# Row sums, low parts, weight conversions and a zero fill moved between engines in an attention, mixture-of-experts and bilinear kernel

## The chip, the core and the metric

The kernel runs on one core of one Trainium2 chip. The metric is the device time of one execution in microseconds (us). Three runs of the kernel before took 779.03, 779.79 and 782.46 us, so the median is 779.79.

## What is computed

The reference chains three layers. The bilinear weights reach the kernel as float64 and are converted in it.

```python
scores = scale * q @ k.T                     # 4 batches, 8 heads, 576 positions, head size 64
scores = where(0 <= rel < 128, scores + slope[h] * -abs(rel), -1e9)
attn = exp(scores - max);  attn /= attn.sum(-1) + 1e-9
x = (attn @ v)  ->  (2304 tokens, 512)
logits = x @ w_gate + modality_bias[modality_id]     # 8 experts, the best one is taken
out[mask] = gate_w[mask] * (relu(x[mask] @ w1[e]) @ w2[e])      # 512 -> 1024 -> 512
a = out @ w1;  b = out @ w2                  # 512 -> 1024 each
result = ((a * b) @ w3) @ w_out              # 1024 -> 1024 -> 512
```

## The kernel before, in words

**Number format.** Products that must be exact are made of split operands. ScalarE writes the high part (a rounded copy, `split` L270), VectorE the low part (source minus high part, L272, or L274 where a factor is applied), and `mm3` (L286 to L289) issues three matmuls: high by high (L287), high by low (L288) and low by high (L289).

**Stages.** From 0 to some 228 us the attention runs. From 262 us on come the experts' blocks and then the bilinear product, in which TensorE is busy nearly without a break. This change concerns the first stage and a few transfers for the second.

**Units.** The attention is cut into 4 batches of 5 chunks (four of 128 positions and a tail of 64), and each chunk into two units of four heads: 40 units, named (batch, chunk, unit). One iteration of the main loop issues scores and softmax of unit i, the transposes of the probabilities of unit i-1 and the product with v of unit i-2, so that three units are in flight. On every second iteration the queries and keys of the next chunk are transposed on TensorE (`transposes_q`, `transposes_k`) and split. The queries of two chunks in turn lie in the tiles qz0 and qz1.

**Low parts on TensorE.** For the chunks with `pe_lo` (of the first nine chunks the eight that aren't tails), the low part is not made by VectorE. TensorE multiplies the high part by a scaled negative identity (L281 for keys, L335 for queries) and adds it to the transposed source in PSUM, and ScalarE copies the rest out (L284, L341).

**Row sums.** The exponentials (L407) also give row sums, in another order of partitions than the tokens have. When the last unit of a chunk is attended, four GpSimd additions (L482) bring the sums of a 128-token tile into token order, `r`; VectorE takes the reciprocal (L486) and `gate_logits` multiplies by it (L511) before the token rows are stored.

**Routing.** Five times, after a group of tiles, `route` finds experts and ranks, and GpSimd issues one indirect DMA per tile (L577) that scatters token numbers into a table in device memory (`inv2`, shown as `inv`).

**Weights in between.** The product of w3 and w_out is worked in between the units: `W_STEPS` says how many steps of it (three matmuls each, `pw`) each unit carries. Their chunks are loaded as float64 words and converted by five VectorE instructions each in `to_f32`: three on words (L697, L701, L704) and two that sum (L707, L710). w_out's eight chunks are due at the units of `WO_AT`, loaded two units before; w3's chunks are loaded `LEAD[0]` units before their first step, converted `LEAD[1]` before and transposed `LEAD[2]` before. Then they are split like the queries.

**Order.** The program text gives each engine's instructions; a scheduler puts them into one order per engine, in which the engine then runs them strictly, each waiting for its semaphores.

**Zero fill.** `fill_rest` writes zeros over `yT`, the device-memory table of the experts' results, with one 128 by 512 tile of zeros, `zf`, one transfer per unit from unit 6 on; the first row of `zf` also becomes the zero row of the token table `xz`.

Of the kernel before, what the change touches and what calls it, by code (L numbers as in the profile page):

```python
# [8 lines left out]
F32 = mybir.dt.float32  # L9
# [9 lines left out]
P = 128  # L19
# [5 lines left out]
NB_MAX = 12  # L25
PE_LO = 9
WO_PRE, W3_PRE = 0, 0
WO_AT = [9, 9, 12, 12, 12, 12, 14, 15]
TP_AFTER = 20
LEAD = [4, 3, 1]  # L30
TS = 384
# [13 lines left out]
def kernel(  # L45
# [63 lines left out]
    ident = const.tile([P, P], F32, tag="ident", name="ident")  # L109
    id_k = a_p.tile([P, P], F32R, tag="id_k", name="id_k", bufs=1)  # L110
    id_q = a_p.tile([P, P], F32R, tag="id_q", name="id_q", bufs=1)
    ones_b = const.tile([P, P], BF16, tag="ones", name="ones_b")
# [65 lines left out]
    def build_constants():  # L178
# [7 lines left out]
        for t in qz[0]:  # L186
            nc.vector.memset(f32(t), 0.0)
        for t, f in ((id_k, -1.0), (id_q, 1.0 / SCALE)):
            nc.vector.tensor_scalar_mul(t, ident, f)

# [86 lines left out]

    def split_pe(hi, lo, tp):

        nc.scalar.activation(out=hi, in_=tp, func=AF.Copy)  # L280
        nc.tensor.matmul(  # L281
            tp, lhsT=id_k, rhs=hi, start=False, stop=True, skip_group_check=True,
        )
        nc.scalar.activation(out=lo, in_=tp, func=AF.Copy)  # L284

    def mm3(dst, lh, ll, rh, rl, start, stop):  # L286
# [9 lines left out]

    def pe_lo(b, c):
        return c < NF and b * (NF + 1) + c < PE_LO

    def head_transposes(nm, b, c, tp, hps):  # L300
        n_t = P if c < NF else TAIL
        t = raw[nm, b, c]
        for hp in hps:
            nc.tensor.matmul(
                tp[:, hp, :n_t],
                lhsT=t[:n_t, 2 * hp : 2 * hp + 2, :].rearrange("p a d -> p (a d)"),
                rhs=ident[:n_t, :n_t], is_transpose=True,
                start=(hp == hps[0] if pe_lo(b, c) else True),
                stop=(hp == hps[-1] or not pe_lo(b, c)),
            )  # L310

    def transposes_q(b, c, hps=range(NP)):
        tp = pst("A", [P, NP, P], f"qtp_{b}_{c}_{hps[0]}")
        head_transposes("q", b, c, tp, hps)
        n_h = 2 if c < NF else 1
        hi, lo = qT[b, c] = qz[(b * (NF + 1) + c) % 2]
        sl = slice(hps[0], hps[-1] + 1)
        parts = []
        for j in range(2):
            r = slice(j * D, (j + 1) * D)  # L320
            if n_h == 2:
                src = tp[r, sl, :].rearrange("p h (s q) -> p (h s) q", s=2)
                dst = [t[r, sl, :, r].rearrange("p h s q -> p (h s) q") for t in (hi, lo)]
            else:
                src = tp[r, sl, :HQ]
                dst = [t[r, sl, 0, r] for t in (hi, lo)]
            parts.append((r, src, *dst))
        if not pe_lo(b, c):
            for r, src, h, l in parts:
                split(h, l, src, scale=-SCALE)  # L330
            return
        for r, src, h, l in parts:
            nc.scalar.activation(out=h, in_=src, func=AF.Copy, scale=-SCALE)
        for j in range(2):
            nc.tensor.matmul(  # L335
                tp[:, sl, :].rearrange("p h (s q) -> p (h s) q", s=2), lhsT=id_q,
                rhs=hi[:, sl, :, j * HQ : (j + 1) * HQ].rearrange("p h s q -> p (h s) q"),
                start=False, stop=j == 1, skip_group_check=True,
            )
        for r, src, h, l in parts:  # L340
            nc.scalar.activation(out=l, in_=src, func=AF.Copy, scale=-SCALE)  # L341

    def transposes_k(b, c, hps=range(NP)):
# [9 lines left out]
        cs = slice(c * P, c * P + n_t)  # L353
        sp = split_pe if pe_lo(b, c) else split
        sp(hi[:, sl, cs], lo[:, sl, cs], tp[:, sl, :n_t])

# [85 lines left out]
    def attend(b, c, hq):  # L442
# [31 lines left out]
        if hq == NQ - 1:  # L474
            st_V.pop((b, c))
            if c < NF or b % 2 == 1:

                sm = sums.pop(i)
                r = a_p.tile([P, NP, 2], F32, tag="r", name=f"r_{b}_{c}", bufs=3)
                for h in range(2):  # L480
                    for j in range(2):
                        nc.gpsimd.tensor_scalar_add(  # L482
                            r[h * HQ : (h + 1) * HQ, :, j], sm[j * HQ : (j + 1) * HQ, h, :], 1e-9
                        )
                r = r.rearrange("p c j -> p (c j)")
                nc.vector.reciprocal(r, r)  # L486
                r_t[i] = r
# [197 lines left out]

    def to_f32(pool, raw_t, name, x=None):

        high = raw_t[:, :, 1]
        low = raw_t[:, :, 0].bitcast(U32)
        n = raw_t.shape[1]  # L690
        w = pool.tile([P, n], I32, tag="d_w", name=f"w_{name}", bufs=2)
        p2 = pool.tile([P, n], I32, tag="d_p", name=f"p_{name}", bufs=1)
        if x is None:
            x = pool.tile([P, HALF], F32, tag="d_x", name=f"x_{name}", bufs=3)

# [10 lines left out]
        )  # L706
        nc.vector.scalar_tensor_tensor(  # L707
            out=x, in0=low, scalar=2.0**-52, in1=p2.bitcast(F32), op0=ALU.mult, op1=ALU.mult
        )
        nc.vector.tensor_tensor(out=x, in0=x, in1=w.bitcast(F32), op=ALU.add)  # L710
        return x
# [8 lines left out]
    def load_wout(g):  # L720
        st_w["o", g] = load_f64(w_p, m_wout[g * P : (g + 1) * P], f"wo_{g}")

    def split_wout(g):
        x = to_f32(w_p, st_w.pop(("o", g)), f"wo_{g}")
        split(woh[:, g, :], wol[:, g, :], x)
# [6 lines left out]

    def cvt_w3(i):
        st_w["x", i] = to_f32(w_p, st_w.pop(("3", i)), f"w3_{i}")

# [61 lines left out]
    def fill_rest():  # L797
# [5 lines left out]
        nc.sync.dma_start(out=ord2.rearrange("(p n) o -> p (n o)", p=P), in_=ni[:, :n])  # L803
        zf = a_p.tile([P, DM], F32, tag="zf", name="zf", bufs=1)
        nc.gpsimd.memset(zf, 0.0)
        nc.sync.dma_start(out=xz[N : N + 1, :], in_=zf[:1, :])
        for j, (d, c) in enumerate((d, c) for c in range(0, NCOL, DM) for d in range(0, DM, P)):
            extras.setdefault(6 + j, []).append(
                lambda d=d, c=c: nc.sync.dma_start(
                    out=yT[d : d + P, c : min(c + DM, NCOL)], in_=zf[:, : min(DM, NCOL - c)]  # L810
                )
            )

# [42 lines left out]
    for g in range(NMC):  # L856
        if g >= WO_PRE:
            at(WO_AT[g] - 2, lambda g=g: load_wout(g))
        at(WO_AT[g], lambda g=g: split_wout(g))
# [51 lines left out]
    if j_in < n_j:  # L911
        load_w3(j_in)
        cvt_w3(j_in)
    if j_in + 1 < n_j:
# [160 lines left out]
    def cvt_m(q, i):  # L1075
# [4 lines left out]
        with tc.issue_after(last["w"].ins):  # L1080
            to_f32(cv_p, wc.pop(("m", q, i)), f"m_{q}_{i}", x=st_w["m"][:, slot, d % 2, :])

# [54 lines left out]
    for n in range(k_in, n_w):  # L1137
        j, first = w_piece(n)
        if first:
# [3 lines left out]
            if j + 1 < n_j:  # L1143
                cvt_w3(j + 1)
        w_step(n)
# [384 lines left out]
```

## Time and profile before

| | |
|---|---|
| Median of three runs | 779.79 us (779.03 to 782.46) |
| The profiled execution | 779.81 us, of which its span is 778.1 |
| Mean granted TensorE clock | 0.983 |
| Busy in the span: TensorE, VectorE, ScalarE, GpSimd | 740.4, 524.1, 363.9, 96.6 us |
| Bytes moved | 116.43 MB |

The shares of the whole span (95 % TensorE, 67 % VectorE) are a mean over stages that differ. The tables by stretch further down give the busy time of each engine in each stretch, with the granted clock as a share of full speed, the mean busy share of the DMA engines and their rate. In the names of rows PE is TensorE, PEld its weight load, DVE VectorE, ACT ScalarE, POOL GpSimd and SP the queue that issues most transfers. Small numbers behind an arrow name what an engine waited for.

### The profile page before, as it was taken

The numbers are of one execution on the slowest core, as the hardware profiler recorded it, in microseconds if no ns is written. First come the engines' busy times: TensorE is split into PE (matmuls) and PEld (weight loads), VectorE is DVE, ScalarE is ACT, GpSimd is POOL, SyncE is SP. The second block draws the span as 40 slices with busy tenths as digits, with TensorE's granted clock in tenths as the row PEclk, the third lists the DMA queues.
The fourth block names the chain that finished last, engine by engine and source line by source line (L and its number), as shares of the span: only waits on it lengthen the run. The fifth ranks groups of instructions, "written<-read, shape, count | busy, mean of one in ns | idle before, by whom it ended". The sixth has DMA issues, their size and how long they took to land. (4 is left out here: it accounts for less than half of the span.)

```text
span 778.1 us, 12375 instructions
## 1 busy us (share of the span) xinstructions
PE 740.4 (95%) x4296; PEld 641.0 (82%) x4296; DVE 524.1 (67%) x1314; ACT 363.9 (47%) x828; POOL 96.6 (12%) x171
## 2 busy tenths in 40 slices
PE   7899898979998999999999999999999999999996
PEld 6778676767876788888888878999789997899974
DVE  4679697737778649698894345788656786567721
ACT  5798776746871433333343435432542225423131
POOL 4100210300313402011020000000120001200011
PEclk9999999969999999999999999999999999999999
DMA  7998366234314857979696435644216332133011
GB/s 135 338 300 215 87 198 163 59 98 130 82 57 85 269 166 210 280 223 326 203 301 187 131 104 179 203 125 131 67 40 203 121 117 75 64 109 119 1 40 42
DMA packets 126166, 116.43 MB, mean 150 GB/s; under 512 B 69596, under 2 KB 100444, under 8 KB 126093
## 3 DMA queue, kind: packets, MB, share of 16 engines
q1 hardware_dynamic: 122477, 105.88, 46.4%
q0 software_dynamic: 3616, 9.66, 3.9%
q8 instruction: 36, 0.59, 0.3%
q14 instruction: 37, 0.30, 0.1%
HBM read 87.85 MB, written 27.68 MB: 148 GB/s over the span
## 5 line engine op out<-in xcount | busy, mean ns | idle before, releaser
L270 ACT ACTIVATE wth<-wt 128x896 fp32r<-128x896 f32 x48 | 43.0, 944 | 89.4 <-PE pP L1276 89.4
L272 DVE TENSOR_TENSOR fwl<-fw,fwh 128x1024 fp32r<-128x1024 f32 x40 | 48.7, 1225 | 52.0 <-ACT fwh L270 51.6
L270 ACT ACTIVATE fwh<-fw 128x1024 fp32r<-128x1024 f32 x40 | 42.2, 1062 | 82.6 <-PE ph L288 65.0
L407 ACT ACTIVATE p<-p,mn 128x192 f32<-128x192 f32 (+2 forms) x144 | 61.7, 431 | 13.6 <-DVE mn L402 13.0
L287 PE MATMUL ph<-xbh,fwh 128*128 128x480 f32 x160 | 61.4, 385 | 1.1 <-issue 0.7
L288 PE MATMUL py<-Whl,fwh 128*128 128x480 f32 x160 | 61.1, 382 | 0.0
L288 PE MATMUL ph<-xbl,fwh 128*128 128x480 f32 x160 | 60.9, 380 | 0.0
L289 PE MATMUL ph<-xbh,fwl 128*128 128x480 f32 x160 | 60.7, 380 | 0.0
L289 PE MATMUL py<-Whl,fwl 128*128 128x480 f32 x160 | 58.8, 379 | 0.0
L287 PE MATMUL py<-Whl,fwh 128*128 128x480 f32 x160 | 57.8, 380 | 0.0
L287 PE MATMUL po<-Whl,abh 128*128 128x512 f32 x144 | 57.2, 397 | 0.6 <-ACT abh L270 0.6
L289 PE MATMUL po<-Whl,abl 128*128 128x512 f32 x144 | 57.2, 398 | 0.0
L288 PE MATMUL po<-Whl,abh 128*128 128x512 f32 x144 | 57.0, 396 | 0.0
L272 DVE TENSOR_TENSOR wtl<-wt,wth 128x896 fp32r<-128x896 f32 x48 | 51.8, 1082 | 4.8 <-ACT wth L270 2.6
L402 DVE CUSTOM_DVE_ANT_0 p<-S,bias 128x192 f32<-128x192 f32 (+2 forms) x144 | 41.4, 329 | 20.1 <-PE S L289 18.3
L1381 POOL DMA_INDIRECT out_dram<-o,sid x18 | 21.6, 1201 | 260.4 <-ACT o L1380 260.4
L272 DVE TENSOR_TENSOR abl<-ab,abh 128x512 fp32r<-128x512 f32 x36 | 24.7, 690 | 41.0 <-ACT abh L270 40.9
L270 ACT ACTIVATE abh<-ab 128x512 fp32r<-128x512 f32 x36 | 22.5, 629 | 58.1 <-PE po L288 40.6
L1285 DVE TENSOR_TENSOR c<-pA,u 128x384 f32<-128x384 f32 x48 | 26.7, 557 | 33.8 <-PE pA L1276 31.6
L468 PE MATMUL av<-pT,vr 128*64 128x128 f32 (+2 forms) x576 | 46.9, 285 | 1.7 <-ACT pT L432 1.2
L468 PEld LDWEIGHTS av<-pT,vr 128*64 128x64 f32 (+1 forms) x576 | 32.3, 142 | 13.5 <-issue 5.7
L422 PE MATMUL PT<-ident,p 128*128 128x128 f32 x208 | 37.7, 299 | 4.5 <-ACT p L407 2.1
(251 smaller groups left out, 2009.0 us busy)
## 6 DMA issues: line engine op xcount, KB each, us to landing
wt<-wT SPq DMA_DIRECT2D x48, 448.0 KB
fw<-in_moe_w_dram SPq DMA_DIRECT2D x40, 512.0 KB
raw_w<-in_moe_w_dram SPq DMA_DIRECT2D x16, 512.0 KB
raw_m<-in_moe_w_dram SPq DMA_DIRECT2D x32, 256.0 KB
wT<-ms SPq DMA_DIRECT2D x16, 448.0 KB
yT<-zf SPq DMA_DIRECT2D x20, 256.0 KB
yT<-y SPq DMA_DIRECT2D x20, 240.0 KB
x<-yT SPq DMA_DIRECT2D x12, 384.0 KB
```

Source lines behind the costliest of these rows:

```text
L270: last["a"] = nc.scalar.activation(out=hi, in_=src, func=AF.Copy, scale=scale)
L272: last["v"] = nc.vector.tensor_tensor(out=lo, in0=src, in1=f32(hi), op=ALU.subtract)
L287: nc.tensor.matmul(dst, lhsT=lh, rhs=rh, start=start, stop=False)
L288: nc.tensor.matmul(dst, lhsT=lh, rhs=rl, start=False, stop=False)
L289: return nc.tensor.matmul(dst, lhsT=ll, rhs=rh, start=False, stop=stop)
L402: nc.vector.tensor_tensor_reduce(out=p[:, t, s, w0:], in0=S_t[s][:, t, w0:], in1=bias[:, hp, w0:], scale=1.0, scalar=BIG, op0=ALU.add, op1 ...
L407: nc.scalar.activation(out=p[:, t, s, w0:], in_=p[:, t, s, w0:], func=AF.Exp, scale=-1.0, bias=m1, accum_out=sm[:, col, hp : hp + 1],)
L422: nc.tensor.transpose(pt[:n, t, x, :], p[:, t, x * P : x * P + n], ident)
L468: nc.tensor.matmul(av[j * D : (j + 1) * D, hp, cs], lhsT=raw["v", b, cc][:n_k, 2 * hp + j, :], rhs=rhs, start=(i_k == 0), stop=(i_k == len ...
L1285: last["d"] = nc.vector.tensor_tensor(out=out, in0=in0, in1=in1, op=op)
L1381: sc = nc.gpsimd.indirect_dma_start(out=out, out_offset=bass.IndirectOffsetOnAxis(ap=sid[g][:, j, 0:1], axis=0), in_=o, in_offset=None, bo ...
```

## The change

Four things are changed, all in the attention stage's code.

1. The four GpSimd additions per tile that bring row sums into token order become two VectorE additions, where source and destination have the same partitions, and two ScalarE copies with an added constant, where they haven't. There are 18 tiles.
2. `split_pe`, `pe_lo` and their identities are gone. All queries and keys go through `split`: high part by ScalarE, low part by VectorE.
3. w_out's chunks are due one per unit, at units 8 to 15; each chunk's conversion (`words_wout`) stands one unit before its split, and its load three units before. w3's loads stand five units ahead and not four. The conversion tiles have one buffer more each (`d_w` 3, `d_p` 2). `to_f32` is cut in two functions; what they issue on VectorE is the same five instructions.
4. `yT` isn't filled with zeros: 24 transfers are gone. The zero row of `xz` comes from a part of a probability tile that stays zero.

```diff
-PE_LO = 9
-WO_AT = [9, 9, 12, 12, 12, 12, 14, 15]
+WO_AT = [8, 9, 10, 11, 12, 13, 14, 15]
-LEAD = [4, 3, 1]
+LEAD = [5, 3, 1]
...
-    def split_pe(hi, lo, tp):
-        nc.scalar.activation(out=hi, in_=tp, func=AF.Copy)
-        nc.tensor.matmul(
-            tp, lhsT=id_k, rhs=hi, start=False, stop=True, skip_group_check=True,
-        )
-        nc.scalar.activation(out=lo, in_=tp, func=AF.Copy)
...
-            parts.append((r, src, *dst))
-        if not pe_lo(b, c):
-            for r, src, h, l in parts:
-                split(h, l, src, scale=-SCALE)
-            return
-        for r, src, h, l in parts:
-            nc.scalar.activation(out=h, in_=src, func=AF.Copy, scale=-SCALE)
-        for j in range(2):
-            nc.tensor.matmul(
-                tp[:, sl, :].rearrange("p h (s q) -> p (h s) q", s=2), lhsT=id_q,
-                rhs=hi[:, sl, :, j * HQ : (j + 1) * HQ].rearrange("p h s q -> p (h s) q"),
-                start=False, stop=j == 1, skip_group_check=True,
-            )
-        for r, src, h, l in parts:
-            nc.scalar.activation(out=l, in_=src, func=AF.Copy, scale=-SCALE)
+            split(*dst, src, scale=-SCALE)
...
-        sp = split_pe if pe_lo(b, c) else split
-        sp(hi[:, sl, cs], lo[:, sl, cs], tp[:, sl, :n_t])
+        split(hi[:, sl, cs], lo[:, sl, cs], tp[:, sl, :n_t])
...
                 for h in range(2):
-                    for j in range(2):
-                        nc.gpsimd.tensor_scalar_add(
-                            r[h * HQ : (h + 1) * HQ, :, j], sm[j * HQ : (j + 1) * HQ, h, :], 1e-9
-                        )
+                    hs, os = (slice(k * HQ, (k + 1) * HQ) for k in (h, 1 - h))
+                    nc.vector.tensor_scalar_add(r[hs, :, h], sm[hs, h, :], 1e-9)
+                    nc.scalar.activation(
+                        out=r[hs, :, 1 - h], in_=sm[os, h, :], func=AF.Copy, bias=1e-9
+                    )
...
-        w = pool.tile([P, n], I32, tag="d_w", name=f"w_{name}", bufs=2)
-        p2 = pool.tile([P, n], I32, tag="d_p", name=f"p_{name}", bufs=1)
+        w = pool.tile([P, n], I32, tag="d_w", name=f"w_{name}", bufs=bufs)
+        p2 = pool.tile([P, n], I32, tag="d_p", name=f"p_{name}", bufs=bufs - 1)
...
+    def words_wout(g):
+        words = words_f32(w_p, st_w.pop(("o", g)), f"wo_{g}", 3)
+        st_w["xo", g] = sum_f32(nc.vector, w_p, words, f"wo_{g}")
...
     def split_wout(g):
-        x = to_f32(w_p, st_w.pop(("o", g)), f"wo_{g}")
+        x = st_w.pop(("xo", g))
         split(woh[:, g, :], wol[:, g, :], x)
...
-        zf = a_p.tile([P, DM], F32, tag="zf", name="zf", bufs=1)
-        nc.gpsimd.memset(zf, 0.0)
-        nc.sync.dma_start(out=xz[N : N + 1, :], in_=zf[:1, :])
-        for j, (d, c) in enumerate((d, c) for c in range(0, NCOL, DM) for d in range(0, DM, P)):
-            extras.setdefault(6 + j, []).append(
-                lambda d=d, c=c: nc.sync.dma_start(
-                    out=yT[d : d + P, c : min(c + DM, NCOL)], in_=zf[:, : min(DM, NCOL - c)]
-                )
-            )
+        nc.sync.dma_start(
+            out=xz[N : N + 1, :].rearrange("o (p c) -> (o p) c", p=4), in_=pTz[0][:4, 0, 1, :]
+        )
...
-            at(WO_AT[g] - 2, lambda g=g: load_wout(g))
+            at(WO_AT[g] - 3, lambda g=g: load_wout(g))
+        at(WO_AT[g] - 1, lambda g=g: words_wout(g))
         at(WO_AT[g], lambda g=g: split_wout(g))
```

Two places show what this makes of the engines' orders. The first is GpSimd around the scatters of the second group, of five tiles (the row sums r_1, r_2 belong to chunks 1 and 2 of batch 2; sums are the row sums as the exponentials left them; inv is the scatters' table). Before:

```order
L482 TENSOR_SCALAR r_1_2136<-sums_1864 64x4 [waits Activation_49]
L482 TENSOR_SCALAR r_1_2136<-sums_1864 64x4
L577 DMA inv_101<-tg,pos_i 19200x2 [waits DVE_49,Pool_49]
L577 DMA inv_101<-tg,pos_i 19200x2 x4
L482 TENSOR_SCALAR r_2_2287<-sums_2040 64x4 [waits Activation_49]
L482 TENSOR_SCALAR r_2_2287<-sums_2040 64x4 [waits DMASW6_49,DMASW5_49,DMASW7_49,DMASW4_49,DMASW0_49]
L482 TENSOR_SCALAR r_2_2287<-sums_2040 64x4 [waits Activation_49]
L482 TENSOR_SCALAR r_2_2287<-sums_2040 64x4
```

On the same engine after the change, the second group's five scatters follow the first group's, and the third group's begin right behind them:

```order
L545 DMA inv_99<-tg,pos_i 19200x2 [waits DVE_49]
L545 DMA inv_99<-tg,pos_i 19200x2 x3
L545 DMA inv_99<-tg,pos_i 19200x2 [waits DMASW0_49]
L545 DMA inv_99<-tg,pos_i 19200x2 [waits DMASW1_49,DVE_49]
L545 DMA inv_99<-tg,pos_i 19200x2 [waits DMASW2_49]
```

Before, the second addition of the row sums waits for five DMAs of GpSimd's own queue, the scatters; after, no row sum stands on that engine.

The second place is VectorE between the last softmax instruction of unit (0,2,1) and the first of unit (0,3,0) (w, p and x are the words, the power of two and the float32 value of a chunk of float64 weights, with _wo for w_out; wol is a low part of w_out, qz1l a low part of queries, lh and x<-xlg the gate's products and token rows; L402 is the softmax's first instruction). Before, from the first row behind the softmax of (0,2,1):

```order
L710 TENSOR_TENSOR x_wo_865<-x_wo_865,w_wo_863 128x512
L272 TENSOR_TENSOR wol<-x_wo_855,woh 128x512
L511 TENSOR_TENSOR lh_574<-xlg_0_575,r_1_554 128x32
L511 TENSOR_TENSOR x_573<-xlg_0_575,r_1_554 128x256
L511 TENSOR_TENSOR lh_574<-xlg_1_580,r_1_554 128x32
L511 TENSOR_TENSOR x_573<-xlg_1_580,r_1_554 128x256
L517 TENSOR_REDUCE lsum_585<-lh_574 128x8
L402 ISA p_3_0_604,mn_3_0_605<-S_3_0_0_589,bias 128x192
```

After the change 25 instructions stand in that place, with softmax now at L369; these are the last of them:

```order
L662 TENSOR_SCALAR w_wo_964<-raw_wo_788 128x512
L687 TENSOR_TENSOR x_wo_785<-x_wo_785,w_wo_780 128x512
L269 SCALAR_TENSOR_TENSOR qz1l<-qtp_3_0_472,qz1h 64x8x64
L669 TENSOR_SCALAR p_wo_852<-w_wo_851 128x512
L454 RECIPROCAL r_2_679<-r_2_679 128x8
L485 TENSOR_REDUCE lsum_564<-lh_553 128x8
L666 SCALAR_TENSOR_TENSOR w_wo_964<-raw_wo_788,w_wo_964 128x512
L662 TENSOR_SCALAR w_w_1_978<-raw_w_1_790 128x512
L267 TENSOR_TENSOR wol<-x_wo_785,woh 128x512
L681 SCALAR_TENSOR_TENSOR x_wo_856<-raw_wo_715,p_wo_852 128x512
L486 TENSOR_TENSOR logit_413<-lsum_564,bmod 128x8
L369 ISA p_3_0_587,mn_3_0_588<-S_3_0_0_572,bias 128x192
```

Before, seven instructions stand between two units' softmax there; after, 25, among them queries' low parts and parts of the conversions of three chunks of w_out and two of w3.

## Rows read from the trace of the kernel before

**Rows 1.** Busy time by stretch (first column its start and end).

```profile
core 0: us, PE busy (x) PEld busy (x) DVE busy (x) ACT busy (x) POOL busy (x), PEclk, DMA share, GB/s
0.00:36.00 36.00, 28.10 (x157) 23.54 (x158) 19.82 (x72) 23.78 (x70) 10.93 (x48) 0.95 0.85 223
36.00:92.00 56.00, 51.32 (x441) 42.83 (x440) 41.33 (x166) 47.02 (x144) 8.86 (x20) 0.97 0.77 214
92.00:129.00 37.00, 34.04 (x262) 26.44 (x261) 33.78 (x111) 25.01 (x77) 4.27 (x12) 1.00 0.63 178
100.00:120.00 20.00, 18.98 (x151) 14.61 (x152) 19.27 (x60) 13.68 (x45) 2.80 (x8) 1.00 0.67 190
...
162.30:175.00 12.70, 12.70 (x68) 11.95 (x69) 6.14 (x28) 7.47 (x26) 0.87 (x4) 0.52 0.33 84
...
262.00:778.00 516.00, 504.50 (x2501) 446.25 (x2499) 337.36 (x571) 187.49 (x277) 43.34 (x37) 1.00 0.47 147
```

**Rows 2.** Waits, 0 to 262 us: total us, times, longest.

```profile
DVE r L486 <- POOL r L482: 14.7, 8, 7.4
POOL r L482 <- DMA inv<-tg,pos_i: 12.6, 3, 6.5
```

**Rows 3.** Timeline from 160 us: start, duration; brackets hold idle time and releaser.

```profile
160.03 0.78 POOL L482 TENSOR_SCALAR r<-sums 64x4 f32<-64x4 f32 x3 [6.53 <-DMA inv<-tg,pos_i]
160.85 0.20 DVE L486 RECIPROCAL r<-r 128x8 f32<-128x8 f32 x1 [7.43 <-POOL r L482]
...
161.63 0.59 ACT L270 ACTIVATE qz1h<-qtp 64x512 fp32r<-64x512 f32 x1 [5.53 <-DVE qz1l L274]
...
162.28 0.53 PE L287 MATMUL S<-kTh,qz1h 128*128 128x192 f32 x1 [4.99 <-ACT qz1h L270]
```

**Rows 4.** Timeline of TensorE around low parts near 18 us and 40 us.

```profile
18.26 0.73 PE L281 MATMUL ktp<-kTh,id_k 128*128 128x512 f32 x1
...
19.64 0.57 PE L287 MATMUL S<-kTh,qz1h 128*128 128x192 f32 x2
...
39.63 0.64 PE L335 MATMUL qtp<-qz1h,id_q 128*128 128x512 f32 x2
40.11 0.49 PE L422 MATMUL PT<-ident,p 128*128 128x128 f32 x3
```

**Rows 5.** Groups by form, 0 to 262 us: busy us, mean ns, idle before.

```profile
L482 POOL TENSOR_SCALAR r<-sums 64x4 f32<-64x4 f32 x64 | 18.2, 284 | 156.4 <-ACT p L407 141.5 <-DMA inv<-tg,pos_i 12.6
...
L701 DVE SCALAR_TENSOR_TENSOR w_w<-raw_w,w_w 128x512 int32<-128x512 int32 x16 | 10.9, 684 | 0.2
...
L704 DVE TENSOR_SCALAR p_w<-w_w 128x512 int32<-128x512 int32 x16 | 6.8, 425 | 0.1
...
L272 DVE TENSOR_TENSOR kTl<-ktp,kTh 128x512 fp32r<-128x512 f32 x8 | 5.4, 679 | 0.9 <-ACT kTh L270 0.8
L341 ACT ACTIVATE qz1l<-qtp 64x512 fp32r<-64x512 f32 x8 | 4.7, 589 | 0.0
L541 ACT ACTIVATE ex<-dd 128x32 f32<-128x32 f32 x2 | 0.4, 216 | 0.0
L567 DVE TENSOR_SCALAR smx<-smx 128x4 f32<-128x4 f32 x2 | 0.3, 158 | 0.0
```

**Rows 6.** Timeline of VectorE, to 92 us, instructions on weights and softmax.

```profile
28.38 0.43 DVE L697 TENSOR_SCALAR w_w<-raw_w 128x512 int32<-128x512 int32 x1 [1.90 <-DMA raw_w<-in_moe_w_dram]
...
31.41 0.68 DVE L710 TENSOR_TENSOR x_w<-x_w,w_w 128x512 f32<-128x512 f32 x1
32.01 0.19 DVE L486 RECIPROCAL r<-r 128x8 f32<-128x8 f32 x1
...
35.96 0.36 DVE L402 CUSTOM_DVE_ANT_0 p<-S,bias 128x192 f32<-128x192 f32 x1 [0.72 <-PE S L289]
...
91.50 0.34 DVE L402 CUSTOM_DVE_ANT_0 p<-S,bias 128x192 f32<-128x192 f32 x1
```

**Rows 7.** Transfers issued, from the page's last part.

```profile
yT<-zf SPq DMA_DIRECT2D x20, 256.0 KB
```

More of the change, by code (lines that the diff above doesn't have):

```diff
@@ L109 @@
     ident = const.tile([P, P], F32, tag="ident", name="ident")
-    id_k = a_p.tile([P, P], F32R, tag="id_k", name="id_k", bufs=1)
-    id_q = a_p.tile([P, P], F32R, tag="id_q", name="id_q", bufs=1)
     ones_b = const.tile([P, P], BF16, tag="ones", name="ones_b")
@@ L187, in build_constants @@
             nc.vector.memset(f32(t), 0.0)
-        for t, f in ((id_k, -1.0), (id_q, 1.0 / SCALE)):
-            nc.vector.tensor_scalar_mul(t, ident, f)
         nc.gpsimd.iota(rel_i, pattern=[[-1, W]], base=P, channel_multiplier=1)
@@ L295 @@
     qT = {}
-    def pe_lo(b, c):
-        return c < NF and b * (NF + 1) + c < PE_LO
     def head_transposes(nm, b, c, tp, hps):
@@ L307, in head_transposes @@
                 rhs=ident[:n_t, :n_t], is_transpose=True,
-                start=(hp == hps[0] if pe_lo(b, c) else True),
-                stop=(hp == hps[-1] or not pe_lo(b, c)),
+                start=True, stop=True,
             )
@@ L317, in transposes_q @@
         sl = slice(hps[0], hps[-1] + 1)
-        parts = []
         for j in range(2):
@@ L684, in load_f64, with words_f32 @@
         return t
-    def to_f32(pool, raw_t, name, x=None):
+    def words_f32(pool, raw_t, name, bufs):
         high = raw_t[:, :, 1]
-        low = raw_t[:, :, 0].bitcast(U32)
         n = raw_t.shape[1]
-        w = pool.tile([P, n], I32, tag="d_w", name=f"w_{name}", bufs=2)
-        p2 = pool.tile([P, n], I32, tag="d_p", name=f"p_{name}", bufs=1)
-        if x is None:
-            x = pool.tile([P, HALF], F32, tag="d_x", name=f"x_{name}", bufs=3)
+        w = pool.tile([P, n], I32, tag="d_w", name=f"w_{name}", bufs=bufs)
+        p2 = pool.tile([P, n], I32, tag="d_p", name=f"p_{name}", bufs=bufs - 1)
         nc.vector.tensor_scalar(
@@ L706, in to_f32, with sum_f32 @@
         )
-        nc.vector.scalar_tensor_tensor(
-            out=x, in0=low, scalar=2.0**-52, in1=p2.bitcast(F32), op0=ALU.mult, op1=ALU.mult
-        )
-        nc.vector.tensor_tensor(out=x, in0=x, in1=w.bitcast(F32), op=ALU.add)
+        return raw_t, w, p2
+    def sum_f32(eng, pool, words, name, x=None):
+        raw_t, w, p2 = words
+        low = raw_t[:, :, 0].bitcast(U32)
+        if x is None:
+            x = pool.tile([P, HALF], F32, tag="d_x", name=f"x_{name}", bufs=3)
+        if eng is nc.vector:
+            eng.scalar_tensor_tensor(
+                out=x, in0=low, scalar=2.0**-52, in1=p2.bitcast(F32), op0=ALU.mult, op1=ALU.mult
+            )
+        else:
+            eng.tensor_scalar(out=x, in0=low, scalar1=2.0**-52, scalar2=None, op0=ALU.mult)
+            eng.tensor_tensor(out=x, in0=x, in1=p2.bitcast(F32), op=ALU.mult)
+        eng.tensor_tensor(out=x, in0=x, in1=w.bitcast(F32), op=ALU.add)
         return x
@@ L731, in load_w3, with cvt_w3 @@
         )
-    def cvt_w3(i):
-        st_w["x", i] = to_f32(w_p, st_w.pop(("3", i)), f"w3_{i}")
+    def cvt_w3(i, eng=nc.vector):
+        words = words_f32(w_p, st_w.pop(("3", i)), f"w3_{i}", 3)
+        st_w["x", i] = sum_f32(eng, w_p, words, f"w3_{i}")
     def w3_transposes(i):
@@ L803, in fill_rest @@
         nc.sync.dma_start(out=ord2.rearrange("(p n) o -> p (n o)", p=P), in_=ni[:, :n])
-        zf = a_p.tile([P, DM], F32, tag="zf", name="zf", bufs=1)
-        nc.gpsimd.memset(zf, 0.0)
-        nc.sync.dma_start(out=xz[N : N + 1, :], in_=zf[:1, :])
-        for j, (d, c) in enumerate((d, c) for c in range(0, NCOL, DM) for d in range(0, DM, P)):
-            extras.setdefault(6 + j, []).append(
-                lambda d=d, c=c: nc.sync.dma_start(
-                    out=yT[d : d + P, c : min(c + DM, NCOL)], in_=zf[:, : min(DM, NCOL - c)]
-                )
-            )
+        nc.sync.dma_start(
+            out=xz[N : N + 1, :].rearrange("o (p c) -> (o p) c", p=4), in_=pTz[0][:4, 0, 1, :]
+        )
     halves = [(slice(0, H // 2), range(NP // 2)), (slice(H // 2, H), range(NP // 2, NP))]
@@ L912 @@
         load_w3(j_in)
-        cvt_w3(j_in)
+        cvt_w3(j_in, nc.vector)
     if j_in + 1 < n_j:
@@ L1080, in cvt_m @@
         with tc.issue_after(last["w"].ins):
-            to_f32(cv_p, wc.pop(("m", q, i)), f"m_{q}_{i}", x=st_w["m"][:, slot, d % 2, :])
+            words = words_f32(cv_p, wc.pop(("m", q, i)), f"m_{q}_{i}", 2)
+            sum_f32(nc.vector, cv_p, words, f"m_{q}_{i}", x=st_w["m"][:, slot, d % 2, :])
     def sum_m(q, i):
@@ L1143 @@
             if j + 1 < n_j:
-                cvt_w3(j + 1)
+                cvt_w3(j + 1, nc.vector)
         w_step(n)
```

## The prediction

> **What bounds the kernel now.** I read the table of stretches first. From 262 us to the end TensorE is busy for 504.50 of 516.00 us at a clock of 1.00 [rows 1]. What the change moves all lies before that, and the instructions of these later stages stand in the same order in both kernels, so I cost them at nothing and carry whatever the attention gains or loses through to the end, us for us. The attention is not one regime. From 0 to 36 us no engine is busy for more than 28.10 us and the DMA engines for 0.85 of the time. From 36 to 92 us TensorE's matmuls are busy for 51.32 of 56 us, ScalarE 47.02, VectorE 41.33: TensorE leads and VectorE has 14.7 us to spare. From 92 to 129 us TensorE has 34.04 of 37 and VectorE 33.78; inside it, from 100 to 120 us, VectorE is at 19.27 of 20.00, a share of .964. That is the best share that VectorE reaches, and shows what it looks like as the bound.
>
> The list of waits then shows a stall of another kind [rows 2]: VectorE waits 14.7 us in all for GpSimd's row sums, and GpSimd, three times, 12.6 us for the scatters' DMAs. The timeline at 160 us shows the longest [rows 3]. GpSimd waits 6.53 us for scatters before it writes r, VectorE's reciprocal has then waited 7.43 us, behind it stands a low part of queries, behind that ScalarE's next high part (5.53 us late), and so TensorE stands idle for 4.99 us. What follows is dearer than the wait: from 162.30 to 175.00 us the granted clock is 0.52 (the 1.2 GHz level), with TensorE busy in every one of the 12.70 us [rows 1].
>
> **Row sums off GpSimd.** Removed are 72 GpSimd additions of some 284 ns [rows 5], and with them the place where a row sum queues behind scatters. Nothing that anyone waits for is then left behind the scatters in the order. At 160 us the 4.99 us of idle time go. If TensorE doesn't stand idle there, the clock need not fall: 12.70 us of work at 0.52 is 12.70 x 0.52 = 6.6 us at full clock, 6.1 us less. Together -11.1 us. What is late next: the reciprocal now waits for ScalarE, which carries half of the additions behind its exponentials. Added are 36 VectorE additions of some 158 ns and 36 ScalarE ones of some 216 ns (the nearest rows, L567 and L541, are of like width [rows 5]), 5.7 and 7.8 us in all. Spread over 18 tiles they are 0.75 us a tile; VectorE and ScalarE have room behind the stall (6.14 and 7.47 of 12.70 us busy [rows 1]), so I charge +1, between 0 and 2. So this stretch gives -10, with ends at -12 (nothing is charged and the idle time's tail goes too) and -4 (only the idle time goes).
>
> **Low parts off TensorE.** TensorE loses 27 matmuls, one for each group of ScalarE's copies: nine for keys and eighteen for queries, seven and fourteen of them 512 wide. Three of them take 19.64 - 18.26 = 1.38 us at the early clock, and two take 40.11 - 39.63 = 0.48 us at full clock [rows 4], 0.24 each. ScalarE loses 27 copies of up to 589 ns. VectorE gains 27 low parts; the full-width ones, 679 ns each [rows 5], start 32.01 - 31.41 = 0.60 us apart where another instruction of this size is followed at once [rows 6]. These are not added to the path one by one; they count in the stages' sums below.
>
> **Conversions.** The five instructions per chunk are the same, and only their place changes, in the order of VectorE. Before the first softmax instruction of unit (0,2,0) five instructions with two inputs (684 ns) and three with one (425 ns [rows 5]) fewer stand now: 3.4 + 1.3 = 4.7 us. Between that point and unit (1,2,0) 21 and 14 more stand. I take these counts from the orders of both kernels, the times from the trace.
>
> **The start, 0 to 35.96 us** (first softmax of unit (0,2,0) [rows 6]). VectorE gets twelve low parts of half or full width and four additions, some 6.6 + 0.6 us, and loses the 4.7 us of conversions and a wait of 1.90 us for a raw weight [rows 6]: level. TensorE loses the equal of six full-width low parts at half clock, 2 x 1.38 = 2.8 us, and two ScalarE copies that stood in the same chain go with each set. The zero fill is 20 transfers of 256 KB and four of half that, 5.8 MB [rows 7] (the four by the size of their tile in the program), issued from unit 6 on, when the stretch moves 223 GB/s with the engines 0.85 busy [rows 1]; 5.8 MB at that rate are 26 us of transfer time that no longer compete with loads. Its issues leave SP's queue too. How much of it was late for anyone the trace shows only at the 1.90 us. Bounds: 0 if all this was hidden, and -7 if TensorE's 2.8, the 1.9 and some 2.3 (half of the conversions) all count; I take -4, near the row that is seen in full.
>
> **36 to 92 us.** Here the sign of the change is decided. VectorE gets twelve full-width low parts and 21 conversions of two inputs, 33 x 0.60 = 19.8 us by starts; 14 with one input, 14 x 0.425 = 6.0; eight additions, 8 x 0.158 = 1.3. That is 27.1 us, and 29.7 by durations (33 x 0.68). VectorE then has 41.33 + 27 = 68.3 us of work between two points that lay 91.50 - 35.96 = 55.5 us apart [rows 6]. TensorE's 51.32 and ScalarE's 47.02 both sink, so VectorE is the bound. At its share of .964 the stretch takes 68.3 / .964 = 70.9 us, +15.4. In this sum the short wait for row sums inside the stretch is already gone. Bounds: 66.7 us at a share of 1.00 and 1.6 us fewer, +11; 68.3 / .85 = 80.4, +25, if the low parts' chain (ScalarE's high part, VectorE's low part, ScalarE's second, VectorE's second, as both write the same tile) leaves holes like that at 100 to 120 us four times over.
>
> Here a row and a page can be weighed. By matmul busy time TensorE fills 51.32 of 56 us, but its weight loads only 42.83 [rows 1]. The Trainium skill ("Trainium Kernel Development and Optimization", Best Practices) holds matmul busy time to be a bad measure, because matmuls are pipelined, and the share of weight loads a good one. By the first, TensorE had 4.7 us of room before, by the second 13.2; by the second, the matmuls taken away here were hidden, and the whole of VectorE's +15.4 stands against nothing. The sum above is made without either.
>
> **92 to 129 us.** The conversions that went ahead are missing here: some 11 us of VectorE's 33.78 go (counts from the orders, times as above). VectorE then has 22.8 us, and TensorE is next: its matmuls are busy for 34.04 of 37.0 us, its weight loads for 26.44 [rows 1]. So the gain lies between 37.0 - 34.0 = 3 and 37.0 - 26.4 = 10.6; I take -7, the middle, as the rows give no nearer one.
>
> **Sum.** -4 + 15.4 - 7 - 11.1 + 1 = -5.7. The profiled execution took 779.81 us with a span of 778.1, within 0.02 of the median 779.79, so I predict 779.8 - 5.7 = 774.1, rounded 774. All dear ends together give 0 + 25 - 3 - 4 = +18, all cheap ends -7 + 11 - 10.6 - 12 = -19; neither is likely as a whole.
>
> **Rivals.**
>
> *No change of note: the clock falls anyway.* The idle 4.99 us are gone, but another wait (the reciprocal behind ScalarE's exponentials) comes in the same place, and the stretch at 0.52 stays. Then -4 + 15.4 - 7 - 5.0 + 1 = +0.4, 780.2. For it: VectorE's order is strict, and ScalarE, at 47.02 of 56 us [rows 1], often runs late. Against: ScalarE loses more than it gets, and a row sum on it waits for exponentials alone, not for a DMA.
>
> *Slower: VectorE as the bound.* Place: 36 to 92 us. The work is put there, and a share of .85 in place of .964 gives 80.4 us, so that the sum becomes -4 + 25 - 7 - 10.1 = +3.9, 783.7; with a start that gains only 1, 786.7. I price it at 785. It decides from a share of about .90: 68.3 / .90 = 75.9 us, +20.4, eats all of the other 21.1 less 0.7. For it: 41.33 us before held many waits, and in a 20 us stretch with the same mix the share .964 was seen only once. Against: conversions wait for nothing but their loads, and fill holes.
>
> *Slower: the clock in the VectorE-bound stretch.* TensorE, left with some 45 to 50 us of work in 70, has gaps again and again; if each makes the clock fall as the one at 160 us did, two such stretches of 12.7 us cost 2 x 6.1 = 12.2 us, of which the bound by VectorE hides a third: +8, 782. For it stands the row at 0.52 behind one gap of 4.99 us; against it the stretch from 100 to 120 us, bound by VectorE, at 1.00 [rows 1]. The Trainium skill ("TensorE: Matmul & The Clock Gate", HAM oscillation) tells of kernels whose repeated waits let the clock fall each time and speaks for this rival; the rows at 100 to 120 us do not agree with it.
>
> **How the numbers follow.** About 0.5 %, 3.9 us, is what can be told from no change here: 775.9 to 783.7 is the same. My forecast has .50, with an own range of 767 to 778; .40 of it lies below 775.9 and .10 above. The clock that falls anyway has .17 and is the same. VectorE at .85 has .25, the clock in its stretch .08, both counted as slower, as their ranges lie about and above 783.7. Faster .40, same .27, slower .33. The range 765 to 790 leaves some .1 on either side out: below, if every term gains at its end but one; above, if the share falls under .80.
>
> **What would show it.** In the profile after: no L482, and the scatters of GpSimd with nothing behind them; around 160 us no idle time of TensorE over 2 us, and no stretch at a half clock behind it. VectorE busy for 65 us or more between the first softmax of unit (0,2,0) and that of (1,2,0), and these about 71 us apart; 80 or more would be the rival. The stretch from (1,2,0) to (2,0,0) shorter by some 7 us, with TensorE leading. The stretch from 262 us on the same length as before within 1 us. If that changes, the argument fails at its first step.

## The result, and the profile after

Five runs of the kernel after gave 784.26 to 789.33 us, median 785.21; five of the kernel before on the same chip 776.40 to 782.46, median 779.03. The ratio is 1.0089 (95 % interval 1.0060 to 1.0119): slower by 0.9 %, where 774 and faster had been forecast. The profiled execution after has a span of 783.4 us.

The forecast's stretches, cut at the same four points (VectorE's first softmax instruction of units (0,2,0), (1,2,0), (2,0,0) and (3,4,0)), compare as follows; each of the two columns of times is one profiled execution.

| Stretch | before | after | change | forecast |
|---|---|---|---|---|
| start to (0,2,0) | 35.96 | 29.46 | -6.5 | -4 |
| to (1,2,0) | 55.54 | 68.82 | +13.3 | +15.4 |
| to (2,0,0) | 37.26 | 33.16 | -4.1 | -7 |
| to (3,4,0) | 97.23 | 93.38 | -3.8 | -10.1 |
| to the end | 552.11 | 558.58 | +6.5 | 0 |
| sum | 778.10 | 783.41 | +5.3 | -5.7 |

The first three rows together were forecast at +4.4 and came to +2.7. The fault lies in the last two. The table of stretches of the kernel after answers to [rows 1]; its columns are the same:

```profile
core 0: us, PE busy (x) PEld busy (x) DVE busy (x) ACT busy (x) POOL busy (x), PEclk, DMA share, GB/s
0.00:29.46 29.46, 22.64 (x124) 20.29 (x125) 20.59 (x73) 17.53 (x58) 8.17 (x39) 1.00 0.82 176
29.46:98.28 68.82, 53.29 (x438) 44.30 (x436) 65.79 (x221) 45.35 (x145) 1.54 (x2) 0.90 0.64 166
98.28:131.44 33.16, 31.84 (x255) 26.44 (x255) 25.73 (x99) 24.16 (x77) 2.77 (x3) 1.00 0.55 128
131.44:224.82 93.38, 85.94 (x763) 72.37 (x763) 65.99 (x297) 72.80 (x252) 8.63 (x9) 1.00 0.45 100
237.00:241.50 4.50, 0.41 (x2) 0.00 (x0) 2.02 (x11) 0.21 (x1) 0.00 (x0) 0.78 0.33 76
241.50:250.00 8.50, 7.79 (x26) 5.92 (x27) 5.22 (x29) 1.21 (x3) 1.91 (x2) 0.51 0.20 62
```

In the second row VectorE is busy for 65.79 of 68.82 us, a share of .956: it is the bound, as forecast. In the fourth the clock is 1.00 throughout, so the stretch at half clock of [rows 1] is gone. The last two rows show TensorE all but idle for 4.5 us at 237 us, then 8.5 us at half clock. The kernel before has a smaller stall at the same place, the last routing step: TensorE waits 1.00 us there, and 3.5 us at half clock follow.

```profile
240.26 0.18 PE L559 MATMUL rk<-hot_b,tri_b 128*128 128x16 bf16 x1 [1.00 <-DVE hot_b L550]
```

```profile
243.00:246.50 3.50, 3.50 (x11) 2.68 (x10) 2.14 (x13) 0.00 (x0) 2.01 (x2) 0.53 0.52 137
```

The waits show why it grew (VectorE, 0 to 262 us, answering to [rows 2]):

```profile
engine line waited for: us in total, times, longest us
DVE w_w L662 <- DMA raw_w<-in_moe_w_dram: 14.5, 9, 3.7
DVE kTl L267 <- ACT kTh L265: 6.8, 7, 1.8
DVE lh L479 <- PE xlg L473: 5.9, 10, 1.8
DVE r L449 <- ACT p L374: 5.0, 9, 1.4
```

The 14.7 us for GpSimd's row sums have gone (5.0 us for ScalarE's exponentials stand ahead of the new row sums), and 14.5 us for loads of float64 weights have come. Before, VectorE had one such wait, 1.90 us [rows 6]. The timeline of one of the two longest, on VectorE and on the queue SP:

```profile
151.37 0.69 DVE L681 SCALAR_TENSOR_TENSOR x_w<-raw_w,p_w 128x512 f32<-128x512 uint32 x1
...
158.64 0.43 DVE L662 TENSOR_SCALAR w_w<-raw_w 128x512 int32<-128x512 int32 x1 [3.63 <-DMA raw_w<-in_moe_w_dram]
...
159.71 0.20 DVE L454 RECIPROCAL r<-r 128x8 f32<-128x8 f32 x1
```

```profile
152.09 0.35 SPq L651 DMA_DIRECT2D raw_w<-in_moe_w_dram  x1
```

L681 is the last reader of a load tile. 0.03 us after its end, at 152.09, the load of a later chunk into that tile is issued, and the next conversion in VectorE's order is of that very chunk: it stands 3.63 us, with the reciprocal behind it. The same happens at 193 us (3.65 us) and again from 236 to 239 us. There the last routing step is queued behind the conversion (VectorE, then TensorE):

```profile
236.02 0.17 DVE L486 TENSOR_TENSOR logit<-lsum,bmod 128x8 f32<-128x8 f32 x1
239.41 0.43 DVE L662 TENSOR_SCALAR w_w<-raw_w 128x512 int32<-128x512 int32 x1 [3.23 <-DMA raw_w<-in_moe_w_dram]
239.76 0.16 DVE L505 TENSOR_REDUCE mx<-logit 128x2 f32<-128x16 f32 x1
...
241.31 0.17 DVE L518 TENSOR_TENSOR hot_b<-iota_em,mnx 128x16 bf16<-128x16 f32 x1
```

```profile
241.54 0.19 PE L527 MATMUL rk<-hot_b,tri_b 128*128 128x16 bf16 x1 [4.13 <-DVE hot_b L518]
```

The last token's logits are ready at 236.2 us, but their maximum (L505) is taken at 239.76, behind a conversion that it has nothing to do with. TensorE waits 4.13 us for the routing's result, and the clock falls as it did at 162 us before.

Why does the order put the conversion there? The orders of both kernels tell. Both have three load tiles. Before, there were two word tiles (`d_w`); the words of chunk j+2 could be made only when chunk j was summed, and the load for it had long been issued, when chunk j-1 gave its tile free. With three word tiles the words of chunk j+3 may follow as soon as chunk j is summed, but that chunk's load waits for the same event. For the last seven chunks of w3, 27 to 106 VectorE instructions stand between a load tile's last reader and the first conversion from it in the kernel before, and by its trace 8.3 to 31.9 us; in the kernel after, 5 to 14 instructions and 3.7 to 7.3 us, the waits included. The count alone sets no threshold: at 114 and 118 us the kernel before has 16 and 18 instructions there, 6.8 and 6.5 us, and no wait.

### The profile page after: what moved, and what is told of

It is laid out like the page before. It is cut to its first block, busy times and chain, and to the rows that moved or that the text cites. A ratio compares the mean times of both kernels' runs of the same rounds, so it can differ in the third digit from the quotient of the medians.

```text
span 783.4 us, 12247 instructions
## 1 busy us (share of the span) xinstructions
PE 734.5 (94%) x4269; PEld 637.7 (81%) x4269; DVE 542.4 (69%) x1375; ACT 358.1 (46%) x837; POOL 72.9 (9%) x98
## 5 line engine op out<-in xcount | busy, mean ns | idle before, releaser
L435 PE MATMUL av<-pT,vr 128*64 128x128 f32 (+2 forms) x576 | 45.1, 277 | 8.5 <-ACT pT L399 4.7
L369 DVE CUSTOM_DVE_ANT_0 p<-S,bias 128x192 f32<-128x192 f32 (+2 forms) x144 | 41.4, 329 | 3.9 <-PE S L276 3.3
```

Source lines behind the costliest of these rows:

```text
L369: nc.vector.tensor_tensor_reduce(out=p[:, t, s, w0:], in0=S_t[s][:, t, w0:], in1=bias[:, hp, w0:], scale=1.0, scalar=BIG, op0=ALU.add, op1 ...
L435: nc.tensor.matmul(av[j * D : (j + 1) * D, hp, cs], lhsT=raw["v", b, cc][:n_k, 2 * hp + j, :], rhs=rhs, start=(i_k == 0), stop=(i_k == len ...
```

## The experiments

Three theories are told apart: **W**, the word tiles let the order run up against the loads; **B**, VectorE is the bound from 36 to 92 us; **P**, the new places of the conversions and their loads. Wherever the word tiles go from three to two or back, the power tiles go from two to one or back with them; "word tiles" stands for both, and which of the two decides isn't shown. Ratios are to the kernel before in runs on the same chip. On the three chips of these runs that kernel took 781.3 to 781.6 us.

**Word tiles back to two.**

```diff
-        words = words_f32(w_p, st_w.pop(("o", g)), f"wo_{g}", 3)
+        words = words_f32(w_p, st_w.pop(("o", g)), f"wo_{g}", 2)
-        words = words_f32(w_p, st_w.pop(("3", i)), f"w3_{i}", 3)
+        words = words_f32(w_p, st_w.pop(("3", i)), f"w3_{i}", 2)
```

> The kernel after, with its word tiles of the weight conversions back at two buffers and its powers at one, as before the change (load tiles three in both); nothing else differs. Theory W (waits for loads): with three word tiles on three load tiles, the order lets VectorE ask for a chunk right after the load tile it lands in came free, so VectorE stands 14.5 us for loads before 262 us, three times 3.2 to 3.7 us, the last time ahead of the last routing step. Expects these waits under 3 us in all and 775 to 780 us. Rival B (VectorE is the bound from 36 to 92 us, by low parts and conversions put there): the waits may go, but the time stays at 784 to 787. Rival P (placement: w_out one per unit, w3 loaded five units ahead): 784 to 787 as well.

773.67 us, ratio 0.9896 (0.9862 to 0.9931). VectorE has one wait left for such a load:

```profile
engine line waited for: us in total, times, longest us
...
DVE w_wo L662 <- DMA raw_wo<-in_moe_w_out_dram: 1.1, 1, 1.1
```

The size of these buffers decides the sign: 1.9 % between this and the kernel after. W holds; B and P, by which the time would stay, fall as the whole cause.

**Four load tiles, word tiles at three.** `load_f64(..., bufs=3)` becomes `bufs=4`.

> The kernel after with four load tiles in place of three for the float64 weights, word tiles at three as in the kernel after. Theory W: the loads are issued one chunk earlier, so VectorE's waits for loads fall from 14.5 us to under 3 and the time to 775 to 780 us, like the run with two word tiles. Rivals B and P: 784 to 787. If this one falls and the run with two word tiles doesn't, the number of loads in flight counts and not the distance in the order.

778.95 us, ratio 0.9968 (0.9948 to 0.9987). The waits go here too (0.5 us left), and some 9 us of the kernel after with them. But 5 us are missing against the run with two word tiles, and the stretch to (1,2,0) shows where (first this kernel, then the one with two word tiles):

```profile
29.63:98.72 69.09, 55.95 (x439) 45.83 (x438) 67.28 (x223) 45.54 (x145) 3.36 (x4) 0.88 0.67 171
```

```profile
30.13:93.31 63.18, 54.39 (x440) 44.49 (x439) 62.52 (x215) 44.78 (x145) 0.99 (x1) 0.89 0.67 174
```

VectorE is the bound in both (67.28 of 69.09, 62.52 of 63.18). With three word tiles the order pulls more conversions into it: 223 VectorE instructions in place of 215, among them nine more of conversions. So the third word tile costs twice: by late loads, and by work drawn into the stretch that VectorE bounds; in the second part B was right.

**Low parts back on TensorE**, as the diff of the change reversed in `transposes_q`, `transposes_k` and `split_pe`.

> The kernel after with the low parts of the first eight full chunks' queries and keys back on TensorE and ScalarE, and nothing else undone. Rival B: VectorE loses 27 low parts, some 17 us of work, most of it in the stretch from (0,2,0) to (1,2,0), which falls from 68.8 us towards 60; 775 to 779 us. Theory W: that stretch gets shorter by some 5 to 8 us at most, but the waits for loads at 155, 193 and 236 us and what follows them stay; 779 to 784.

792.28 us, ratio 1.0153 (1.0115 to 1.0192): neither theory's number. The stretch to (1,2,0) does shrink, from 68.8 to 66.7 us, but the waits for loads double:

```profile
DVE w_w L695 <- DMA raw_w<-in_moe_w_dram: 28.9, 11, 7.1
```

With word tiles at three this comparison says little of low parts; it is repeated with two below.

**Row sums back on GpSimd**, the four additions of before in `attend`.

> The kernel after with the row sums back as four GpSimd additions per tile. If the removed stall was worth what the prediction said of its stretch (10 us), 793 to 796 us, with TensorE idle again behind row sums around 150 to 165 us and a stretch at the lower clock. If the gain was only the 3.8 us that the stretch from (2,0,0) to (3,4,0) really lost, 787 to 791. If ScalarE's half of the sums makes up for it: 784 to 787.

792.52 us, ratio 1.0162 (1.0130 to 1.0195): 0.7 % slower than the kernel after by the first ratio of that kernel (1.0089), some 6 us, and 0.6 % by its later one (1.0102, below), whose interval overlaps this one. As a difference this is the second case (2 to 6 us); the time itself lies between the first two. The waits for loads (12.7 us) and for row sums (13.2 us) stand side by side in it.

**The kernel before with three word tiles and nothing else.**

```diff
-        w = pool.tile([P, n], I32, tag="d_w", name=f"w_{name}", bufs=2)
-        p2 = pool.tile([P, n], I32, tag="d_p", name=f"p_{name}", bufs=1)
+        w = pool.tile([P, n], I32, tag="d_w", name=f"w_{name}", bufs=3)
+        p2 = pool.tile([P, n], I32, tag="d_p", name=f"p_{name}", bufs=2)
```

> The kernel before with three word tiles and two power tiles for the weight conversions in place of two and one, nothing else. Theory W: VectorE's order then asks for chunks of w3 right behind the load tile's release here too (6 to 15 instructions between the two late in the attention, where before has 26 to 104), so VectorE waits for loads, about 10 us in all, also ahead of the last routing step: 785 to 791 us where before is 779 to 781. If the waits need the other changes too (w_out one per unit, low parts on VectorE): 778 to 783.

791.23 us, ratio 1.0119 (1.0072 to 1.0166). The tiles alone make the kernel before as much slower as the whole change did; the intervals overlap. The edit reaches the conversions of the bilinear product too, which the change left at two tiles, but the bilinear product takes 289.4 us in the profiles with and without it. The waits, in a profile of the slowest of its six runs (799.1 us):

```profile
DVE r L486 <- POOL r L482: 20.4, 7, 9.8
...
DVE w_w L697 <- DMA raw_w<-in_moe_w_dram: 13.4, 6, 5.3
```

Shown from both sides, then: taken out of the kernel after, and put into the kernel before. The loads are not all of it here: VectorE's waits for the row sums grew too, from 14.7 to 20.4 us.

**Two word tiles, and one part undone each.** These three have the first experiment's edit and the reversal named.

Low parts back on TensorE:

> The kernel after with two word tiles, as in the run that took 773.7 us, and the low parts of the first eight full chunks back on TensorE and ScalarE. If moving low parts to VectorE gains (its 27 instructions fit beside others, TensorE's 27 and ScalarE's 27 don't): slower than 773.7, 777 to 783. If it costs, as the prediction's stretch from 36 to 92 us has it (+15.4 us, about half of it by low parts): 765 to 770.

776.66 us, ratio 0.9940 (0.9914 to 0.9967). The interval overlaps that without the reversal, so no gain or loss is shown. The stretch to (1,2,0) takes 55.2 us in place of 63.2, the one from the start to (0,2,0) 37.4 in place of 30.1: the low parts on VectorE give ahead of (0,2,0) what they take behind it. The zero fill is absent from both, so what the start gained comes from the low parts.

Row sums back on GpSimd:

> The kernel after with two word tiles, and the row sums back as GpSimd additions. The prediction puts the row sums' move at 10.1 us (the idle time at 160 us and the clock behind it, less 1 us): 782 to 786. With three word tiles the same step cost about 4 us: 777 to 779 if that is what it is worth.

779.90 us, ratio 0.9970 (0.9932 to 1.0008), about 6 us slower than without the reversal, between the two expectations; the two intervals only just part.

Zeros back:

> The kernel after with two word tiles, and the 24 transfers of zeros back. If these transfers (5.8 MB from 20 to 44 us) delay loads that VectorE or TensorE wait for, 777 to 781. If they ran beside everything: 773 to 775, with the first units where they are without them.

778.20 us, ratio 0.9947 (0.9911 to 0.9984), overlapping; inconclusive. In its profile the unit (3,4,0) starts at 218.5 us, against 216.2 without the zeros; the start to (0,2,0) takes 29.5 us, against 30.1, so the zeros delayed nothing there.

**The kernel after once more, as it is.**

> The kernel after as it is, beside the next three on one chip, so that they can be set against it. All theories: 1.006 to 1.012 of the kernel before, and again over 10 us of VectorE's waits for loads of float64 weights before 262 us.

792.41 us, ratio 1.0102 (1.0057 to 1.0148), with 19.5 us of waits for loads. In this profile the stretch from (2,0,0) to (3,4,0) took 100.7 us where the first profile has 93.4. Its two waits for loads are longer there, 4.25 and 5.05 us in place of 3.63 and 3.65, and behind them the clock fell, which it did not in the first profile (the whole stretch, then a part of it):

```profile
159.42 0.43 DVE L662 TENSOR_SCALAR w_w<-raw_w 128x512 int32<-128x512 int32 x1 [4.25 <-DMA raw_w<-in_moe_w_dram]
```

```profile
161.91 0.35 PE L274 MATMUL S<-kTh,qz1h 128*128 128x192 f32 x1 [1.97 <-ACT qz1h L265]
```

```profile
131.59:232.28 100.69, 92.80 (x764) 78.94 (x763) 65.85 (x298) 73.43 (x252) 8.63 (x9) 0.92 0.43 93
165.00:175.00 10.00, 10.00 (x60) 9.43 (x59) 4.05 (x22) 6.58 (x24) 0.00 (x0) 0.55 0.42 102
```

**Two word tiles and four load tiles.**

> The kernel after with two word tiles and four load tiles; the instructions' order is that of the run with two word tiles and three load tiles. Theory W: with two word tiles no load was late any more, so a fourth load tile brings nothing: within 0.4 % of that run (a ratio of 0.986 to 0.994 to the kernel before). If the loads in flight were the scarce thing by themselves, under 0.985.

774.50 us, ratio 0.9905 (0.9869 to 0.9941): as with three load tiles. Where the order leaves time for a load, one more tile for it brought nothing.

**The conversions' old places.** Word tiles at two, and:

```diff
-WO_AT = [8, 9, 10, 11, 12, 13, 14, 15]
+WO_AT = [9, 9, 12, 12, 12, 12, 14, 15]
-LEAD = [5, 3, 1]
+LEAD = [4, 3, 1]
...
-            at(WO_AT[g] - 3, lambda g=g: load_wout(g))
-        at(WO_AT[g] - 1, lambda g=g: words_wout(g))
+            at(WO_AT[g] - 2, lambda g=g: load_wout(g))
+        at(WO_AT[g], lambda g=g: words_wout(g))
```

> The kernel after with everything on the weight conversions as before the change: w_out due at units 9, 9, 12, 12, 12, 12, 14, 15 and loaded two units before, w3 loaded four units ahead, two word tiles; row sums, low parts and zeros as in the kernel after. If the new places of the conversions were worth something: over 776 us, a ratio above 0.994. Theory W holds only the word tiles guilty and the places for nearly nothing, since the order moves by three instructions or fewer: a ratio of 0.986 to 0.994.

780.45 us, ratio 0.9981 (0.9951 to 1.0011). W's expectation missed: the new places are worth some 0.8 %, with the new low parts and row sums in place. They are a gain, so P is not what made the kernel after slower. In the one profile this kernel reaches (3,4,0) at 217.2 us, against 216.2 with the new places, and loses 3.1 us behind it. Why it is slower there stays open.

**The kernel before with the row sums moved, and nothing else.**

> The kernel before with the row sums moved from GpSimd to VectorE and ScalarE, and nothing else. The prediction's step says -10.1 us, 769 to 773 (a ratio of 0.985 to 0.990). By what the row sums cost when put back into the kernel after (about 4 to 6 us): 774 to 778 (0.992 to 0.996). If another wait takes the stall's place: a ratio of 0.997 to 1.003.

770.73 us, ratio 0.9864 (0.9829 to 0.9900), the fastest of all. Its stretches, cut as in the table above:

```profile
0.00:36.37 36.37, 29.64 (x162) 24.88 (x163) 20.32 (x76) 24.80 (x75) 8.66 (x40) 1.00 0.86 221
36.37:89.91 53.54, 48.70 (x416) 41.19 (x414) 42.03 (x173) 48.08 (x150) 4.21 (x4) 0.97 0.77 221
89.91:127.10 37.19, 34.26 (x285) 27.90 (x284) 34.61 (x118) 27.05 (x84) 0.00 (x0) 1.00 0.66 182
127.10:214.82 87.72, 83.21 (x736) 69.97 (x735) 66.06 (x297) 72.53 (x251) 9.12 (x9) 1.00 0.51 106
```

The first three stretches are those of the kernel before within 2 us (36.0, 55.5, 37.3); the fourth takes 87.72 in place of 97.23, at a clock of 1.00. By the ratio the step is worth 10.6 us, where the prediction has 10.1. It and the kernel after with two word tiles (0.9896; 0.9905 with four load tiles) are the fastest of the versions run; their intervals overlap.

## Why the prediction was wrong

The step that failed is the one on conversions, in its first sentence: "The five instructions per chunk are the same, and only their place changes, in the order of VectorE." The third word tile was in the diff and in the description of the change, and got no term of its own, and the rival on VectorE was marked down with "conversions wait for nothing but their loads, and fill holes". They do wait for their loads. How long depends on how far ahead a load can be issued, and that is set by the load tiles less the word tiles in flight: one chunk before, none after. The orders of both kernels, which were at hand ahead of any run, show it: 5 to 14 instructions in place of 27 to 106 for the last seven chunks. The second step that failed is the first of the prediction, that from (3,4,0) on nothing is gained or lost: +6.5 us, of which only a part comes from the third word tile (the last part of this section).

What this cost, by the experiments: the kernel after without the third word tile has 0.9896 where it has 1.0089 with it, 0.0193 x 779.8 = 15 us (10 to 20 by the ends of the intervals). The two profiles lie 11.1 us apart: 5.6 in the stretch to (1,2,0), by the conversions drawn into it, 4.4 in the one to (3,4,0), where the two long waits stand, 2.5 behind that, and 1.4 the other way.

Without the third word tile the forecast's 774.1 (a ratio of 0.9927) lies inside the measured interval, but that is luck. In that kernel's profile the five stretches change by -5.8, +7.6, -3.4, -8.3 and +4.0 us, where -4, +15.4, -7, -10.1 and 0 were forecast; the errors cancel in the sum.

The steps one by one:

- Row sums: right for the kernel before, where the step alone gives 10.6 us (8 to 13 by the interval) for 10.1. Put back into the kernel after with two word tiles, they cost about 6. In the kernel after the stretch gave back only 3.8: two waits for loads, 3.63 and 3.65 us, lie in it. In the later profile of the same kernel it took 3.5 us more than before, with the clock at 0.55 behind a load's wait: in that execution the rival that the clock falls anyway came true, behind a load and not behind the exponentials. With two word tiles the stretch takes 88.97 us, 8.3 less than before.
- Start: -6.5, inside the bounds of 0 and -7, more than the -4 taken. The cause was mis-sized: with two word tiles the low parts alone make 7.3 us of difference here (37.4 to 30.1), where 2.8 were counted for them, and the zeros, put back, cost the start nothing (29.5 us).
- 36 to 92 us: +13.3 for +15.4, with VectorE at a share of .956 for the .964 assumed. The conversions in this sum were counted in the order of the kernel after, so they hold those that the third word tile drew in; with two word tiles the stretch grew by 7.6 us only, and by 10.3 in the run with four load tiles. The clock in it was 0.90: it fell, as the rival on the clock had it, but that this cost time isn't shown. From 40 to 60 us it was 0.83, with VectorE busy for 19.72 of 20 us:

```profile
40.00:60.00 20.00, 15.65 (x122) 13.25 (x123) 19.72 (x65) 13.44 (x43) 0.00 (x0) 0.83 0.68 191
```

- 92 to 129 us: -4.1 for -7, inside the bounds of -3 and -10.6. TensorE's matmuls are busy for 31.84 of 33.16 us, its weight loads for 26.44; the gain came out near the bound that was set by the matmuls (-3). That TensorE bounds this stretch isn't shown by that.
- From (3,4,0) on: forecast 0, measured +6.5. That the experts' and the bilinear instructions stand in the same order doesn't make them take the same time; the parts are below.

Cut at the first matmul of the last routing step (rk) and at the first matmul of the experts (ph), the last stretch took, in us:

| Part | before | after | after, two word tiles |
|---|---|---|---|
| (3,4,0) to rk | 14.27 | 16.72 | 14.29 |
| rk to ph | 29.94 | 31.79 | 33.66 |
| ph to the end | 507.90 | 510.07 | 508.17 |

The first part grew by the third wait (4.13 us of TensorE in place of 1.00). With two word tiles it is as before, with a wait of 1.01 us:

```profile
230.47 0.18 PE L527 MATMUL rk<-hot_b,tri_b 128*128 128x16 bf16 x1 [1.01 <-DVE hot_b L518]
```

In the second part half a clock stands behind the third wait, but with two word tiles the part is longer still. The third part, which the prediction held to 1 us, grew by 2.2; its clock is 0.83 from 270 to 280 us, where before has 1.00. Why, stays open in both. The whole stretch takes 556.1 us with two word tiles and 553.2 in the run with four load tiles, whose order on VectorE is the same. So of the +6.5 the third word tile accounts for something between 2.5 and 5.3.

Of the rivals, "slower: VectorE as the bound" gave nearly the right time (785) for another reason: its share of .85 was not seen.

## What to carry to other kernels

Count tiles along a chain of buffers, not each for itself: a deeper ring for an intermediate result lets a scheduler use up the slack of the ring that feeds it, and an engine that runs in strict order then stands for a load with everything else queued behind it. Measure in the order how many instructions lie between the release of a tile and the next use of what is loaded into it. When several edits come together, price the edit that only changes a buffer count as well; here it outweighed the others.

## What the runs showed of the hardware

One load of 512 KB of float64 words took 6.5 us from issue to the conversion behind it at 152 us (issued at 152.09, read at 158.64). Waits of TensorE of 4.99 and 4.13 us were followed by half a clock at 162 us before and at 241 us after (0.51 over 8.5 us). Shorter ones were too: in the later profile of the kernel after a wait of 1.97 us, ahead of 165 us (0.55 over 10 us), and in its first profile, from 40 us on, no single wait of over 1.83 us. There the clock of 0.83 is made of a stretch near the lower level (1.2 GHz) between two at the full one (2.4 GHz), with TensorE busy for 3.11 of the 5 us ahead of the fall:

```profile
40.00:45.00 5.00, 3.11 (x30) 2.48 (x31) 4.88 (x15) 1.97 (x5) 0.00 (x0) 1.00 0.72 203
45.00:52.00 7.00, 5.49 (x31) 5.30 (x30) 6.94 (x25) 4.30 (x15) 0.00 (x0) 0.51 0.75 183
52.00:60.00 8.00, 7.05 (x66) 5.47 (x65) 7.91 (x28) 7.18 (x24) 0.00 (x0) 1.00 0.60 190
```
